# An immediate for the quarter turn of 768 sines, in place of a [128,1] operand

## The chip, the cores and the metric

The kernel runs on one core of one Trainium2 chip. The metric is device microseconds of one execution of the program, as the median of several runs. The time before was 840.31 us (three runs, 839.6 to 840.46). The sets of rounds ran on different chips, so each time is set against the kernel before in its own rounds.

In the profile the engines are called PE (TensorE, matmuls), PEld (TensorE's weight loads), DVE (VectorE), ACT (ScalarE), POOL (GpSimd) and SP (SyncE, whose queue issues most DMAs). L359 is line 359 of the kernel's file. "idle before, releaser" is the time an engine stood before an instruction, and what ended most of it.

## The reference

```python
def _attn_ref(x, filt_r, filt_i):                  # x: 8 x 3008 x 256
    X = np.fft.rfft(x, axis=1)
    Y = X * (filt_r + 1j * filt_i)[None, :, :]
    return np.fft.irfft(Y, n=x.shape[1], axis=1).astype(np.float32)

def _moe_ref(x, w_in, w_out, alpha):               # x: 24064 x 256, 2048 hidden
    h = x @ w_in
    s = np.sin(alpha * h)
    g = h + s * s / (alpha + 1e-09)
    return (g @ w_out).astype(np.float32)
```

A spectral filter along the sequence is followed by a two-layer network whose activation is the "snake" function. As sin² is (1 − cos)/2, the kernel needs the cosine of the scaled hidden value, and takes it as the sine of that value plus a quarter turn.

## The kernel before

The spectral filter of a batch is three stages of matmuls with table matrices. Stage 1 makes `pa` from x. Stage 2 makes `pb`, a product with the filter, and `pc`. Stage 3 makes `pd`. Each of these results stands in PSUM until ACT or DVE evicts it: `pa` to `t`, `pb` to `xf`, `pc` to `g`, `pd` to `y`. For batches 1 to 7 they all share a pool of two PSUM buffers (`fps`). Of the evictions to `t`, `g` and `y`, every third goes to the DVE and two thirds to ACT.

The network works on chunks of up to 512 tokens. A chunk has eight steps. A step holds four hidden matmuls (`ph`, two tiles of 128x512), a piece of the next batch's spectral work, and eight output matmuls (`po`) of the chunk before.

```python
    fps = pool("fps", 2, PSUM)
    hps = pool("hps", 4, PSUM)
    ops = pool("ops", 2, PSUM)
    # ... cut ...
    def evac(dst, src, on_act=None):
        flip[0] = (flip[0] + 1) % 3
        if flip[0] if on_act is None else on_act:
            marks["act"] = nc.scalar.copy(out=dst, in_=src)
        else:
            marks["dve"] = nc.vector.tensor_copy(out=dst, in_=src)
    # ... cut ...
    quarter = cpool.tile([128, 1], FP32)
    nc.vector.memset(quarter, float(np.pi / 2))
    # ... cut: in hidden(k, jb), after the two matmuls into ps ...
        cs = cospool.tile([128, 512], FP32, name=f"cos_{k}_{jb}", tag="c")
        nc.scalar.activation(out=cs[:, 0:n], in_=ps[:, 0:n], func=AFT.Sin, bias=quarter)
        marks["snake"] = nc.vector.scalar_tensor_tensor(
            out=v[k][:, jb, 0:n], in0=cs[:, 0:n], scalar=-1.0, in1=ps[:, 0:n],
            op0=ALU.add, op1=ALU.subtract)
    # ... cut: the main loop ...
        for j in range(8):
            if k < len(chunks):
                hidden(k, 2 * j)
                hidden(k, 2 * j + 1)
            if k == 0:
                weights_out(j)
            while pending and pending[0][0] <= step:
                pending.pop(0)[2]()                       # the spectral pieces
            if k > 0:
                n_half = 2 * (chunks[k - 1][2] // 128)
                for u in range(n_half * j // 8, n_half * (j + 1) // 8):
                    project(k - 1, u)                     # eight output matmuls
            step += 1
```

The program is traced in this order, and a scheduler then decides the order of each engine's instructions, by its own estimate of how long each takes.

Of the kernel before, what the change touches and what calls it, by code (L numbers as in the profile page):

```python
# [10 lines left out]
FP32 = mybir.dt.float32  # L11
AFT = mybir.ActivationFunctionType
# [42 lines left out]
def kernel(  # L55
# [10 lines left out]
    nc = tc.nc  # L66
# [17 lines left out]
    def pool(name, bufs, space=None):  # L84
        kw = {} if space is None else {"space": space}
        return ctx.enter_context(tc.tile_pool(name=name, bufs=bufs, **kw))

    cpool = pool("consts", 1)
# [149 lines left out]
    warm = cpool.tile([128, 1], FP32)  # L238
    nc.vector.memset(warm, 0.0)
    nc.scalar.activation(out=warm, in_=warm, func=AFT.Sin)  # L240
    quarter = cpool.tile([128, 1], FP32)
    nc.vector.memset(quarter, float(np.pi / 2))

    first = spectral(0)
    for _, piece in first[:8]:
# [12 lines left out]
    for i in range(2):  # L258
        al_row.append(opool.tile([128, 2, C], FP32, name=f"al_row_{i}", tag="o"))
        for h in range(2):  # L260
            nc.scalar.dma_start(
                out=al_row[i][64 * h:64 * h + 1].rearrange("p a b -> p (a b)"),
                in_=moe_alpha.rearrange("(k a j) -> k a j", k=4, a=1)[2 * i + h])
# [9 lines left out]
    for g in range(4):  # L273
        for k, filt in enumerate((filt_r, filt_i)):
            for q in range(2):
                off, step = ((6 * g) * C, C) if q == 0 else ((N1 - 6 * g) * C, -C)
                ins = nc.gpsimd.dma_start(
                    out=f_t[k][32 * q:32 * q + 32, 6 * g:6 * g + 6, :],
                    in_=bass.AP(tensor=filt.tensor, offset=filt.offset + off,
                                ap=[[N1 * C, 32], [step, 6], [1, C]]))  # L280
# [18 lines left out]
    ps = fps.tile([128, 512], FP32, name="ps_rec", tag="f")  # L299
# [24 lines left out]
    for i in range(4):  # L324
        for cb in range(2):
            behind(nc.vector.tensor_tensor(
                out=w1[:, cb, 512 * i:512 * i + 512], in0=w_in32[:, cb, 512 * i:512 * i + 512],
# [21 lines left out]
    def hidden(k, jb):  # L349

        _, c0, n = chunks[k]
        if jb == 0:
            v[k] = vpool.tile([128, 16, 512], FP16, name=f"v_{k}", tag="v")
        ps = hps.tile([128, 512], FP32, name=f"ph_{k}_{jb}", tag="h")
        for cb in range(2):
            nc.tensor.matmul(out=ps[:, 0:n], lhsT=w1[:, cb, jb * 128:jb * 128 + 128],  # L356
                             rhs=y_cols[:, cb, c0:c0 + n], start=(cb == 0), stop=(cb == 1))
        cs = cospool.tile([128, 512], FP32, name=f"cos_{k}_{jb}", tag="c")
        nc.scalar.activation(out=cs[:, 0:n], in_=ps[:, 0:n], func=AFT.Sin, bias=quarter)  # L359
        marks["snake"] = nc.vector.scalar_tensor_tensor(  # L360
            out=v[k][:, jb, 0:n], in0=cs[:, 0:n], scalar=-1.0, in1=ps[:, 0:n],
            op0=ALU.add, op1=ALU.subtract)
# [49 lines left out]
    for k in range(len(chunks) + 1):  # L412
# [7 lines that stand above are left out]
                pending.pop(0)[2]()  # L420
# [3 lines that stand above are left out]
                    project(k - 1, u)  # L424
            step += 1
# [31 lines left out]
```

## Time and profile before

| | before |
|---|---|
| time | 840.31 us |
| PE busy | 799.2 us, 95% of the span |
| ACT busy | 674.7 us, 80% |
| DVE busy | 628.4 us, 75% |
| cosine of 128x512, mean | 690 ns |

The page of the kernel before: busy time of the engines, the chain of work that ended last, and three of the costliest groups (count, busy us, mean ns of one, then the idle time before them).

```profile
PE 799.2 (95%) x5793; PEld 544.1 (65%) x5793; DVE 628.4 (75%) x1120; ACT 674.7 (80%) x1200; POOL 28.3 (3%) x55
PE 82%; DMA 7%; DVE 4%; ACT 4%; issue 2%; SPq 0%; POOL 0%; ACTq 0%; DVEq 0%; POOLq 0%
...
L360 DVE SCALAR_TENSOR_TENSOR v<-cos,ph 128x512 f16<-128x512 f32 (+1 forms) x768 | 483.8, 671 | 148.1 <-ACT cos L359 147.1
L359 ACT ACTIVATE cos<-ph,quarter 128x512 f32<-128x512 f32 (+1 forms) x768 | 480.6, 680 | 103.9 <-PE ph L356 101.6
L371 PE MATMUL po<-w,v 128*128 128x256 f16 x3008 | 401.3, 273 | 4.2 <-DVE w L339 4.2
```

TensorE sets the time: it is 82% of the chain. ACT waits 101.6 us for `ph`, so it has time left. The groups split by form show the cost of the operand. All three have 128x512 results from PSUM on ACT; only the first reads a [128,1] operand.

```profile
L359 ACT ACTIVATE cos<-ph,quarter 128x512 f32<-128x512 f32 x704 | 446.9, 690 | 94.4 <-PE ph L356 92.1 <-DVE v L360 1.1
L183 ACT CAST xf<-pb 128x512 f16<-128x512 f32 x96 | 56.6, 591 | 8.8 <-DMA t<-d 5.7 <-DVE p L187 2.0 <-PE pb L180 1.0
L377 ACT COPY o<-po 128x512 f32<-128x512 f32 x92 | 54.9, 597 | 8.5 <-PE po L371 7.4
```

Busy time does not tell how near TensorE is to its own limit, for its matmuls overlap: the `po` above has a mean of 273 ns, yet the next one starts 109 ns after it. The Trainium skill says so too ("Perfetto Trace Analysis", section "Identifying the Most-Contended Engine": matmul busy share is not a good measure). This document therefore uses a sum that is not a view of the profile. For every matmul, take the time to the start of the next one on TensorE, less the median of that time for matmuls of the same result (109 ns for `po`, 216 ns for `ph`). Where this is over 25 ns it is called a *delay*. Summed from 80 us after the start, when the start-up is over, the delays before are 13.7 us. Of these, 4.8 us stand before `pc`, in 23 places, and 5.7 us before `pa`. That sum is the most that a faster ACT or DVE could gain after the start-up; 1.7 us of it is one wait for a load. The view of TensorE's waits, over the same stretch, lists only 2.6 us, because a modelled matmul end hides most of a short delay.

Here is one delay before `pc`, in the timeline of the kernel before (start us, length us, engine, line, operation, tiles, count; in brackets the idle time).

```profile
200.84 2.65 DVE L360 SCALAR_TENSOR_TENSOR v<-cos,ph 128x512 f16<-128x512 f32 x4 [0.31 <-ACT cos L359]
...
203.24 1.03 PE L356 MATMUL ph<-y,w 128*128 128x512 f16 x4
203.41 0.75 DVE L187 TENSOR_TENSOR p<-xf,filt 128x512 f16<-128x512 f16 x2
203.88 1.26 ACT L359 ACTIVATE cos<-ph,quarter 128x512 f32<-128x512 f32 x2 [0.65 <-PE ph L356]
204.07 0.68 DVE L137 CAST g<-pc 128x512 f16<-128x512 f32 x1
204.11 0.38 PE L180 MATMUL pb<-t,d_t 128*128 128x256 f16 x2
204.32 0.49 PE L371 MATMUL po<-w,v 128*128 128x256 f16 x3
204.68 1.27 DVE L360 SCALAR_TENSOR_TENSOR v<-cos,ph 128x512 f16<-128x512 f32 x2
204.81 0.60 PE L199 MATMUL pc<-p,e_t 128*128 128x256 f16 x4
```

Three `po` start at 204.32; at 109 ns each TensorE could start `pc` at 204.65. It starts at 204.81, right after the DVE's eviction of `g` (204.07 + 0.68) frees the buffer. That eviction had queued behind the products (`p`), the products behind the snakes (`v`) of two pairs, which end at 203.49, and these snakes had waited 0.31 us for a cosine. So a shorter cosine should pull this chain forward.

### The profile page before, as it was taken

What the parts mean: (1) busy time and instruction counts of PE and PEld (TensorE: products, weight loads), DVE (VectorE), ACT (ScalarE), POOL (GpSimd) and SP (SyncE); (2) the same over time, 40 slices, a digit from 0 to 9 for tenths busy, and PEclk for the clock granted to TensorE, in tenths of its full rate; (3) what the DMA queues carried; (4) which work ended last, traced back from release to release, by engine and by line L of the source; (5) the groups of instructions that cost most, each with busy time, mean ns of one, the idle gap of its engine ahead of it and who ended that gap; (6) DMA issues with size and microseconds to landing.
All of it is one profiled execution on the core that took longest, in us unless ns stands there. A gap on an engine that the chain in (4) does not pass through costs nothing.

```text
span 839.2 us, 16120 instructions
## 1 busy us (share of the span) xinstructions
PE 799.2 (95%) x5793; PEld 544.1 (65%) x5793; DVE 628.4 (75%) x1120; ACT 674.7 (80%) x1200; POOL 28.3 (3%) x55
## 2 busy tenths in 40 slices
PE   6748999999999999999999999999999999999996
PEld 2324676667776676666776677666767677666674
DVE  3658786777877787777877788777877778777772
ACT  4546897888878898888888888888988988788873
POOL 3210000000000000000000000000000000000000
PEclk9978999999999999999999999999999999999999
DMA  9985845184344734367242763447343343421111
GB/s 216 219 252 116 190 98 130 48 182 106 88 133 82 181 86 98 88 128 167 66 126 61 168 136 81 117 87 171 91 97 94 98 113 82 115 57 38 38 39 45
DMA packets 93495, 94.98 MB, mean 113 GB/s; under 512 B 8084, under 2 KB 82852, under 8 KB 93416
## 3 DMA queue, kind: packets, MB, share of 16 engines
q1 hardware_dynamic: 84784, 75.02, 34.4%
q0 software_dynamic: 6704, 18.09, 12.4%
q10 hardware_dynamic: 1928, 0.86, 0.5%
q8 instruction: 45, 0.74, 0.4%
q14 instruction: 34, 0.28, 0.1%
HBM read 58.02 MB, written 49.81 MB: 128 GB/s over the span
## 4 chain that ended last, share of the span: by engine, by line
PE 82%; DMA 7%; DVE 4%; ACT 4%; issue 2%; SPq 0%; POOL 0%; ACTq 0%; DVEq 0%; POOLq 0%
PE ph L356 35%; PE po L371 35%; PE pc L199 5%; PE pa L157 4%; PE pd L219 2%; DMA t<-d 2%; PE pb L180 2%; ACT cos L359 2%; DMA d<-t 1%; DMA w_out<-in_moe_w_out_dram 1%; DVE v L360 1%; DVE p L187 1%; DMA d<-g 1%; ACT t L135 1%; DMA filt<-in_filt_r_dram 1%
## 5 line engine op out<-in xcount | busy, mean ns | idle before, releaser
L360 DVE SCALAR_TENSOR_TENSOR v<-cos,ph 128x512 f16<-128x512 f32 (+1 forms) x768 | 483.8, 671 | 148.1 <-ACT cos L359 147.1
L359 ACT ACTIVATE cos<-ph,quarter 128x512 f32<-128x512 f32 (+1 forms) x768 | 480.6, 680 | 103.9 <-PE ph L356 101.6
L371 PE MATMUL po<-w,v 128*128 128x256 f16 x3008 | 401.3, 273 | 4.2 <-DVE w L339 4.2
L356 PE MATMUL ph<-y,w 128*128 128x512 f16 (+1 forms) x1536 | 391.3, 376 | 0.3 <-ACT y L135 0.2
L371 PEld LDWEIGHTS <-v 128*128 128x128 f16 x3008 | 289.0, 98 | 80.7 <-issue 8.9
L356 PEld LDWEIGHTS <-w 128*128 128x128 f16 x1536 | 150.6, 98 | 102.8 <-issue 5.5
L187 DVE TENSOR_TENSOR p<-xf,filt 128x512 f16<-128x512 f16 x192 | 72.1, 418 | 6.2 <-ACT xf L183 5.4
L377 ACT COPY o<-po 128x512 f32<-128x512 f32 x96 | 56.5, 589 | 9.8 <-PE po L371 7.4
L183 ACT CAST xf<-pb 128x512 f16<-128x512 f32 x96 | 56.6, 591 | 8.8 <-DMA t<-d 5.7
L135 ACT CAST t<-pa 96x512 f16<-96x512 f32 x89 | 50.0, 588 | 16.4 <-PE pa L157 16.4
L199 PE MATMUL pc<-p,e_t 128*128 128x256 f16 x384 | 59.9, 276 | 2.9 <-DVE p L187 1.5
L219 PEld LDWEIGHTS <-t 96*128 96x128 f16 x512 | 35.5, 98 | 39.0 <-DMA t<-d 11.8
L157 PE MATMUL pa<-x,wf_t 94*96 94x512 f16 x128 | 47.6, 410 | 9.7 <-DMA x<-in_x_dram 5.8
L219 PE MATMUL pd<-wi_t,t 96*128 96x94 f16 x512 | 42.3, 207 | 11.1 <-DMA t<-d 10.6
L135 ACT CAST y<-pd 128x376 f16<-128x376 f32 x82 | 38.7, 474 | 12.2 <-PE pd L219 12.2
L199 PEld LDWEIGHTS <-e_t 128*128 128x128 f16 x384 | 37.7, 99 | 15.7 <-issue 7.5
L180 PE MATMUL pb<-t,d_t 128*128 128x256 f16 x192 | 38.2, 283 | 3.5 <-DMA t<-d 2.4
L135 ACT CAST g<-pc 128x512 f16<-128x512 f32 x64 | 38.7, 605 | 2.2 <-PE pc L199 1.9
L137 DVE CAST y<-pd 128x376 f16<-128x376 f32 x46 | 25.2, 548 | 19.3 <-PE pd L219 19.1
L137 DVE CAST t<-pa 96x512 f16<-96x512 f32 x39 | 26.7, 684 | 16.8 <-PE pa L157 16.1
L180 PEld LDWEIGHTS <-d_t 128*128 128x128 f16 x192 | 18.7, 101 | 25.4 <-DMA t<-d 4.5
L118 POOL DMA_DIRECT2D x<-in_x_dram x32 | 16.6, 522 | 504.6 <-PE pa L157 494.0
(29 smaller groups left out, 86.1 us busy)
## 6 DMA issues: line engine op xcount, KB each, us to landing
d<-t SPq DMA_DIRECT2D x32, 384.0 KB
d<-g SPq DMA_DIRECT2D x64, 192.0 KB
t<-d SPq DMA_DIRECT2D x32, 384.0 KB
x<-in_x_dram POOLq DMA_DIRECT2D x32, 376.0 KB, 7.2
t<-d SPq DMA_DIRECT2D x60, 192.0 KB
out_dram<-o SPq DMA_DIRECT2D x72, 94.0 KB
w_in<-in_moe_w_in_dram POOLq DMA_DIRECT2D x2, 1024.0 KB, 9.0
w_out<-in_moe_w_out_dram POOLq DMA_DIRECT2D x1, 2048.0 KB, 12.4
```

The lines of the kernel that those rows point to most:

```text
L135: marks["act"] = nc.scalar.copy(out=dst, in_=src)
L157: marks["pe"] = nc.tensor.matmul(out=ps[0:NK, :], lhsT=wf_t, rhs=st["x"][ch][:, n0:n0 + 2, :], start=True, stop=True)
L180: nc.tensor.matmul(out=ps[:, i, :], lhsT=d_t[:, s, :], rhs=st["t2"][s // 6][:, s % 6, :], start=True, stop=True)
L183: nc.scalar.copy(out=xf, in_=ps)
L187: marks["prod", u] = nc.vector.tensor_tensor(out=pt, in0=xf, in1=f_t[k][:, 2 * u:2 * u + 2, :], op=ALU.mult)
L199: nc.tensor.matmul(out=ps[:, i, :], lhsT=e_t[:, k, 2 * w + i, :], rhs=pr[k][:, i, :], start=(k == 0), stop=(k == 1))
L219: nc.tensor.matmul(out=psv[:, i, :], lhsT=st["t4"][:, 4 * half + i, cb * 128:cb * 128 + 128], rhs=wi_t, start=True, stop=True)
L356: nc.tensor.matmul(out=ps[:, 0:n], lhsT=w1[:, cb, jb * 128:jb * 128 + 128], rhs=y_cols[:, cb, c0:c0 + n], start=(cb == 0), stop=(cb == 1))
L359: nc.scalar.activation(out=cs[:, 0:n], in_=ps[:, 0:n], func=AFT.Sin, bias=quarter)
L360: marks["snake"] = nc.vector.scalar_tensor_tensor(out=v[k][:, jb, 0:n], in0=cs[:, 0:n], scalar=-1.0, in1=ps[:, 0:n], op0=ALU.add, op1=ALU. ...
L371: nc.tensor.matmul(out=pso[k][:, t % 2, :], lhsT=v[k][:, jb, 128 * t:128 * t + 128], rhs=w2[:, jb, :], start=(jb == 0), stop=(jb == 15))
L377: nc.scalar.copy(out=o[:, 0:nb, :], in_=pso[k][:, 0:nb, :])
```

## The change

The operand becomes an immediate, a number within the instruction, so that the instruction no longer reads a [128,1] tile, and the memset goes.

```diff
-    quarter = cpool.tile([128, 1], FP32)
-    nc.vector.memset(quarter, float(np.pi / 2))
...
-        nc.scalar.activation(out=cs[:, 0:n], in_=ps[:, 0:n], func=AFT.Sin, bias=quarter)
+        nc.scalar.activation(out=cs[:, 0:n], in_=ps[:, 0:n], func=AFT.Sin, bias=float(np.pi / 2))
```

The two built programs also differ in their order, although the source order is the same.

## The prediction

> **What bounds the kernel.** The page gives PE 799 of 839 us (95%), ACT 675 (80%), DVE 628 (75%). I summed matmul columns by stretch (groups by form): from 200 to 700 us they fill 96 to 97% of the time at 2400 columns per us. Matmuls there follow each other every 216 ns (512 columns) or 109 ns (256), both also the medians of the run, so TensorE runs at its own rate. The chain of waits says the same: PE is 82% of it, the cosine (ACT, L359) 1.7%.
>
> **What the change does.** It removes the [128,1] operand from 768 ACTIVATEs and one memset. The cosine lasts 687 ns (median); evictions of the same 128x512 from PSUM by the same engine without such an operand last 588 ns. Starts of two cosines in a row are some 575 ns apart, of two evictions 465. The Trainium skill ("ScalarE: Activation LUTs", section "What ACT_TABLE_LOAD costs") says a [128,1] pointer operand adds about 93 ns to an ACTIVATE; the 100 ns between cosine and eviction agrees, though these are different instructions. I expect 585 to 595 ns for the cosine, and some 75 us less ACT busy time, to about 600.
>
> **How much is on the critical path.** Little. I took every matmul start that came over 25 ns later than the usual distance. Before 80 us such delays are the start-up: loads, the half clock granted there, and the wait for the output weights (the DVE stood 4.5 us for that load). The cosine sets none of it but some tenths. After 80 us they come to only 13 us in all: 4.8 us before stage 2's second matmuls (pc), which wait for the DVE's eviction of g; about 5.3 us before stage 1 (pa), waiting for ACT's evictions of y and t queued behind a pair of cosines; 1.7 us for one DMA. They are 0.16 to 0.39 us each. A cosine 0.1 us shorter moves the DVE's chain (snake, products, g) up by 0.1 us and an ACT eviction behind two cosines by 0.2 us. Estimate: 2.5 us less before pc, 2.5 to 3 before pa: 5 to 6 us gained at most.
>
> **What it moves.** The built orders differ: the scheduler thinks the cosine shorter. On the DVE some 25 evictions, mostly of y, now stand behind a pair of snake instructions (1.28 us) where they stood before it. Most harm nothing, as the next use of their buffer is two steps off. Where stage 1 of the next batch overlaps (the y of pd_8 or pd_9 in three batches, and two t), two buffers are shared and the next pa may stand 0.5 to 1 us: an estimate of 2 to 4 us given back. On ACT and PE a few evictions and single matmuls swap near 58 to 95 us and at the overlaps; six stores go behind loads. I expect little of these.
>
> **Predicted:** 838 us, range 834 to 841. Faster by over 2%: 1%; within 2%: 98%; slower by over 2%: 1%.
>
> **What would show it.** Cosine median near 590 ns; ACT busy near 600 us; PE busy share unchanged at 95 to 96%; ACT's wait for ph (101.6 us before) longer by most of the 75 us; PE's delays before pc smaller; delays of 0.5 us or more before some pa, waiting for y on the DVE; start-up to 66 us unchanged.
>
> **What would make it wrong.** The immediate costs as much as the operand (no change at all); the moved evictions cost more than a few us (842 to 846); the granted clock, 0.5 in parts of the start-up, shifts; or delays after 80 us vanish entirely (828), which would still be within 2%.

## The result, and the profile after

The changed kernel took 840.04 us (four runs, 839.21 to 841.37), against 840.38 us of the kernel before (four runs). The ratio is 0.9994, with a 95% interval of 0.9972 to 1.0016. All ratios in this document are made from runs of both kernels in the same rounds; they are not quite the ratio of the medians quoted (e1 below: 0.9919, 0.9908 by the medians).

The page of the changed kernel, the lines that answer to those above:

```profile
PE 799.8 (96%) x5793; PEld 544.2 (65%) x5793; DVE 628.1 (75%) x1119; ACT 613.0 (73%) x1200; POOL 28.3 (3%) x55
PE 83%; DMA 7%; ACT 4%; issue 3%; DVE 2%; POOL 0%; SPq 0%; ACTq 0%; DVEq 0%; POOLq 0%
...
L358 DVE SCALAR_TENSOR_TENSOR v<-cos,ph 128x512 f16<-128x512 f32 (+1 forms) x768 | 484.0, 672 | 164.0 <-ACT cos L357 163.5
L357 ACT ACTIVATE cos<-ph 128x512 f32<-128x512 f32 (+1 forms) x768 | 411.6, 589 | 153.9 <-PE ph L354 152.5
L369 PE MATMUL po<-w,v 128*128 128x256 f16 x3008 | 400.9, 273 | 2.6 <-DVE w L337 2.6
```

And its cosine of 128x512 alone, from the groups by form:

```profile
L357 ACT ACTIVATE cos<-ph 128x512 f32<-128x512 f32 x704 | 383.6, 598 | 140.0 <-PE ph L354 138.6
```

The cosine fell from 690 to 598 ns, to the level of a plain eviction, and ACT's busy time by 61.7 us. Most of that became waiting: ACT's wait for `ph` grew from 101.6 to 152.5 us. TensorE's delays after 80 us went only from 13.7 to 13.1 us. The same delay before `pc` in the changed kernel's timeline:

```profile
201.82 1.03 PE L354 MATMUL ph<-y,w 128*128 128x512 f16 x4
201.89 0.75 DVE L187 TENSOR_TENSOR p<-xf,filt 128x512 f16<-128x512 f16 x2
202.45 1.08 ACT L357 ACTIVATE cos<-ph 128x512 f32<-128x512 f32 x2 [0.83 <-PE ph L354]
202.56 0.68 DVE L137 CAST g<-pc 128x512 f16<-128x512 f32 x1
202.68 0.38 PE L180 MATMUL pb<-t,d_t 128*128 128x256 f16 x2
202.90 0.38 PE L369 MATMUL po<-w,v 128*128 128x256 f16 x2
203.16 1.27 DVE L358 SCALAR_TENSOR_TENSOR v<-cos,ph 128x512 f16<-128x512 f32 x2
203.30 0.60 PE L199 MATMUL pc<-p,e_t 128*128 128x256 f16 x4
```

Measured from the start of `ph`, the DVE's `g` starts 0.74 us later here (202.56 − 201.82) and 0.83 us later before (204.07 − 203.24). So the chain did come 0.09 us earlier, by as much as the cosine is shorter. But only two `po` stand between `pb` and `pc`, not three. TensorE has 0.109 us less work to fill the wait with, and the delay stays: 0.18 us in place of 0.16. The gain may thus be there and have been given back by the new order. The experiments ask whether that is so, how large both sides are, and which engine's order gives it back.

### The profile page after: what moved, and what is told of

It reads as the page before. It is cut to its first block, busy times and chain, and to the rows that moved or that the text cites. A ratio compares the mean times of both kernels' runs of the same rounds, so it can differ in the third digit from the quotient of the medians.

```text
span 837.2 us, 16122 instructions
## 1 busy us (share of the span) xinstructions
PE 799.8 (96%) x5793; PEld 544.2 (65%) x5793; DVE 628.1 (75%) x1119; ACT 613.0 (73%) x1200; POOL 28.3 (3%) x55
## 4 chain that ended last, share of the span: by engine, by line
PE 83%; DMA 7%; ACT 4%; issue 3%; DVE 2%; POOL 0%; SPq 0%; ACTq 0%; DVEq 0%; POOLq 0%
PE po L369 36%; PE ph L354 35%; PE pc L199 4%; PE pa L157 3%; ACT cos L357 2%; PE pd L219 2%; PE pb L180 2%; DMA t<-d 1%; DMA w_out<-in_moe_w_out_dram 1%; DMA d<-g 1%; DMA d_t<-d_tbl 1%; DVE p L187 1%; DMA x<-in_x_dram 1%; DMA filt<-in_filt_i_dram 1%; ACT t L135 1%
## 5 line engine op out<-in xcount | busy, mean ns | idle before, releaser
L357 ACT ACTIVATE cos<-ph 128x512 f32<-128x512 f32 (+1 forms) x768 | 411.6, 589 | 153.9 <-PE ph L354 152.5
L219 PE MATMUL pd<-wi_t,t 96*128 96x94 f16 x512 | 43.4, 208 | 11.1 <-DMA t<-d 10.9
L157 PEld LDWEIGHTS <-wf_t 94*96 94x96 f16 x128 | 16.6, 129 | 19.6 <-issue 9.9
```

The costliest lines, as they stand in the source:

```text
L157: marks["pe"] = nc.tensor.matmul(out=ps[0:NK, :], lhsT=wf_t, rhs=st["x"][ch][:, n0:n0 + 2, :], start=True, stop=True)
L219: nc.tensor.matmul(out=psv[:, i, :], lhsT=st["t4"][:, 4 * half + i, cb * 128:cb * 128 + 128], rhs=wi_t, start=True, stop=True)
```

## The experiments

Theory A: the shorter cosine is worth several us, and the scheduler's new order gives them back. Rival B: these delays hang on a ring of DVE and TensorE work, and the cosine's length hardly matters.

| run | order | cosine | time, us | before in the same rounds | ratio, 95% interval | delays after 80 us: all | before pc | before pa |
|---|---|---|---|---|---|---|---|---|
| before | old | operand | 840.38 | | | 13.7 | 4.8 | 5.7 |
| changed | new | immediate | 840.04 | 840.38 | 0.9994, 0.9972–1.0016 | 13.1 | 4.6 | 6.0 |
| e1 | old | immediate | 833.29 | 841.03 | 0.9919, 0.9904–0.9934 | 6.1 | 1.9 | 2.2 |
| e2 | new | operand | 848.62 | 841.03 | 1.0095, 1.0079–1.0111 | 21.8 | 7.5 | 10.5 |
| e3 | old | two operands | 853.63 | 841.03 | 1.0152, 1.0138–1.0165 | 25.9 | 11.1 | 10.3 |
| e4 | new, g on ACT | immediate | 836.07 | 841.03 | 0.9949, 0.9937–0.9962 | 10.9 | 0.1 | 5.9 |
| e5 | PE old, rest new | immediate | 839.67 | 841.77 | 0.9969, 0.9947–0.9992 | 12.1 | 2.0 | 6.8 |
| e6 | PE new, rest old | immediate | 840.28 | 841.77 | 0.9979, 0.9957–1.0001 | 12.7 | 4.4 | 5.5 |
| e7 | pieces in the middle | immediate | 835.11 | 841.77 | 0.9917, 0.9896–0.9938 | 7.5 | 0.6 | 5.0 |
| e8 | pieces last | immediate | 834.67 | 841.77 | 0.9909, 0.9886–0.9932 | 7.4 | none | 4.3 |
| e9 | as e8 | operand | 837.1 | 840.89 | 0.9955, 0.994–0.997 | 10.5 | none | 7.2 |
| e10 | old, g on ACT | immediate | 831.14 | 840.89 | 0.9889, 0.9869–0.9909 | 5.5 | none | 2.1 |
| e11 | DVE new, rest old | immediate | 837.73 | 841.57 | 0.9957, 0.9939–0.9975 | 11.2 | 2.1 | 6.1 |
| e12 | ACT and DMA new, rest old | immediate | 834.89 | 841.57 | 0.9924, 0.9908–0.994 | 7.4 | 2.0 | 3.3 |

All of them gave correct results. The delays come from one profiled execution each. They account for the times: in these fourteen profiles the span goes from 829.8 to 852.0 us, but the span less the delays only from 823.1 to 826.0 us.

### e1 and e2: the two parts of the change, one at a time

To change the operand without the order, the kernel is scheduled first and the 768 cosines are replaced in the finished program. Every wait and every place in the order stay. For e1 the source is the kernel before:

```diff
+    for f in nc.m.functions:                      # after the scheduler
+        for b in f.blocks:
+            listed = b.instructions
+            for n, i in enumerate(listed):
+                if ...:                           # a Sin of a ph tile: 768 of them
+                    listed[n] = copy.replace(i, ins=(i.ins[0], ImmediateValue(
+                        dtype=FP32, value=float(np.pi / 2)), *i.ins[2:]))
```

For e2 the source is the changed kernel, with the memset of `quarter` and one read of it by an early ACTIVATE kept, and the operand put in. The order of e1 equals that of before on every engine. The order of e2 equals that of the changed kernel, but for the memset and the place of one DMA issue in the start-up.

> The order of before on every engine, with the immediate put into the 768 cosines after the scheduler has run. Theory A (the shorter cosine does shorten TensorE's waits, and the scheduler's new order gives that back: it puts the second matmuls of stage 2 and of stage 1 one or more output matmuls of 109 ns earlier): cosine median 590 ns, TensorE's delays after 80 us down from 13.7 to 7 to 10 us, time 3 to 6 us under before (834.5 to 837.5). Rival B (those waits do not hang on the cosine but on a ring of DVE and TensorE work): delays 12.5 to 13.7 us, time 839 to 841, as the changed kernel.

> The order of the changed kernel, with the [128,1] operand put back into the 768 cosines after the scheduler has run. Theory A: cosine median 687 ns, delays after 80 us of 17 to 20 us, each of stage 2's waits 0.28 in place of 0.18 us, time 842.5 to 846. Rival B: delays near 13 us, time 839 to 841.

Measured: 833.29 us for e1 and 848.62 us for e2. Theory A holds in both, and both sizes were larger than expected. In the old order the immediate is worth 7.7 us (841.03 − 833.29). With the operand the new order costs 7.6 us (848.62 − 841.03). From the ratios and their intervals one gets 6.8 us (5.6 to 8.1) and 8.0 us (6.6 to 9.3), so each size is known to little better than 1 us. The timeline of e1 at the delay shown above:

```profile
199.41 1.03 PE L356 MATMUL ph<-y,w 128*128 128x512 f16 x4
...
200.04 1.09 ACT L359 ACTIVATE cos<-ph 128x512 f32<-128x512 f32 x2 [0.83 <-PE ph L356]
200.15 0.68 DVE L137 CAST g<-pc 128x512 f16<-128x512 f32 x1
...
200.49 0.49 PE L371 MATMUL po<-w,v 128*128 128x256 f16 x3
200.75 1.27 DVE L360 SCALAR_TENSOR_TENSOR v<-cos,ph 128x512 f16<-128x512 f32 x2
200.89 0.60 PE L199 MATMUL pc<-p,e_t 128*128 128x256 f16 x4
```

`g` again starts 0.74 us after `ph`, as in the changed kernel. But three `po` stand before `pc`, as before, so `pc` comes 0.40 us after their first start and the delay is 0.07 us. The 23 delays before `pc` sum to 1.9 us.

### e3: a longer cosine

The old order once more, with the scale of 1 given as a second [128,1] operand, put in after the scheduler in the same way.

```diff
-   ins=(ph, quarter, ImmediateValue(1.0), ...)
+   ins=(ph, quarter, one, ...)                    # one: a [128,1] tile of 1.0
```

> The order of before, and the cosine's scale of 1 as a second [128,1] operand. Theory A: cosine median some 780 ns, each of stage 2's 0.16 us waits becomes about 0.25 us and stage 1's 0.29 about 0.5, delays after 80 us of 19 to 24 us, time 845 to 852. Rival B: time 839 to 841 and delays near 13 us, while ScalarE is busy some 745 us.

Measured: 853.63 us, a little over the expected range, with delays of 25.9 us (19 to 24 expected). The group by form:

```profile
L361 ACT ACTIVATE cos<-ph,quarter,one 128x512 f32<-128x512 f32 x704 | 510.9, 785 | 52.0 <-PE ph L358 48.6 <-DVE w L341 0.5
```

With no, one and two operands the cosine takes 598, 690 and 785 ns, so each operand costs 92 and 95 ns. In the same order of work the time goes 833.29, 841.03, 853.63: the second operand costs 12.6 us and the first 7.7. Two things in the traces go with the larger second step: 34 delays stand before `pc` in place of 23, and two cosines in a row now start 676 ns apart (585 before), so that the second snake of a pair waits for its cosine and the pair lasts 1.36 us in place of 1.27 or 1.28. How much each makes is not shown. Rival B falls.

### e4: the eviction of g moved to ACT

```diff
-                evac(st["g"][:, i0:i0 + 2, :], ps, i0 != 2 if b == 0 else None)
+                evac(st["g"][:, i0:i0 + 2, :], ps, i0 != 2 if b == 0 else True)
```

> The changed kernel with all of stage 2's evictions of g on ScalarE for batches 1 to 7 (before: every third on the DVE). ScalarE has time left after the change. Theory A says the wait of 0.18 us before stage 2's second matmuls, 4.4 us in all, ends with the DVE's eviction of g and so goes; if nothing else comes in its place, time 835 to 837. If ScalarE's queue takes over (cosine pair, xf, g, and o every fourth step), the wait comes back behind an eviction of ScalarE and the time is 839 to 842.

Measured: 836.07 us, inside the lower of the two ranges. The delays before `pc` are gone but for 0.1 us, so they did hang on the DVE's eviction of `g`. The scheduler also moved the `po` here: none is left between `pb` and `pc` in the 23 places, so nothing fills a wait there, and still there is none. Those before `pa` are what they were in the changed kernel (5.9 us).

### e5 and e6: TensorE's order alone

Here the changed kernel is scheduled with a recorded order of some engines. Each instruction is put behind its neighbour by a dependency without a semaphore, which orders the issue only. It adds seven lines ahead of the kernel body, so line numbers shift by seven.

```diff
+    for engine, order in PINNED.items():
+        made = [...]                               # that engine's instructions as traced
+        for n in range(1, len(order)):
+            tc.add_manual_dep(made[order[n]], made[order[n - 1]].name, ...)   # NoSync
```

> The changed kernel with TensorE's order pinned to that of before; DVE, ACT and the DMA queue keep the changed kernel's order. Theory P (what gives the gain back is TensorE's order: pc after two output matmuls in place of three, pa after six in place of seven): 833 to 836, delays after 80 us of 6 to 8 us. Rival D (as predicted before: it is the DVE's evictions of y standing behind a pair of snakes): 838 to 841, delays of 11 us or more with waits for y on the DVE.

> The changed kernel with TensorE's own (changed) order, and DVE, ACT and the DMA queue pinned to the order of before. Theory P: 838.5 to 841, delays after 80 us of 12 to 13.5 us. Rival D: 833 to 836.

Measured: 839.67 us for e5 and 840.28 us for e6. Theory P was right for e6 and wrong for e5; rival D was right for e5 and wrong for e6. So neither alone is the cause: each half of the new order is enough to lose most of the gain, and the two losses do not add. The columns by result show what belongs to which. Of the orders, the delays before `pc` follow TensorE's alone: 4.4 us with the new one (e6), 2.0 with the old (e5). Those before `pa` rise from 2.2 us (e1) with either half: to 5.5 us in e6 and 6.8 us in e5.

### e11 and e12: the other engines, apart

> The changed kernel with only the DVE in its changed order; TensorE, ACT and the DMA queue pinned to the order of before. Theory V (the cost of the non-TensorE part, some 6 us of delays in the run that left only TensorE in the old order, is the DVE's evictions of y and t behind a pair of snakes): delays after 80 us of 10 to 12 us with waits before pa of some 0.44 us, time 837.5 to 840.5. Rival S (it is ACT's order, o and t swapped, or the stores put behind loads): 6 to 7.5 us, 832.5 to 835.

> The changed kernel with ACT and the DMA queue in their changed order; TensorE and DVE pinned to the order of before. Theory V: delays after 80 us of 6 to 7.5 us, time 832.5 to 835. Rival S: delays of 10 to 12 us, time 837.5 to 840.5.

The edit is that of e5, with other engines named. Measured: 837.73 us and delays of 11.2 us with the DVE's new order alone, 834.89 us and 7.4 us with the new order of ACT and of the DMA queue. Theory V was right for both. So the larger part of what e5 lost is the DVE's doing, some 5.1 us of delays (11.2 − 6.1), and the orders of ACT and the DMA queue cost at most 1.3 us of delays. The times agree in direction: by the ratios e11 lies 0.38% over e1 and e12 only 0.05%. The timeline of e11 where the evictions of stage 3 meet stage 1:

```profile
172.41 0.33 PE L226 MATMUL pd<-wi_t,t 96*128 96x94 f16 x4
172.58 0.38 PE L164 MATMUL pa<-x,wf_t 94*96 94x512 f16 x1
172.80 0.71 PE L376 MATMUL po<-w,v 128*128 128x256 f16 x5
172.81 1.28 DVE L365 SCALAR_TENSOR_TENSOR v<-cos,ph 128x512 f16<-128x512 f32 x2 [0.89 <-ACT cos L364]
173.15 0.58 ACT L142 CAST t<-pa 96x512 f16<-96x512 f32 x1
173.78 0.38 PE L164 MATMUL pa<-x,wf_t 94*96 94x512 f16 x1 [0.27 <-ACT t L142]
...
174.01 0.54 DVE L144 CAST y<-pd 128x376 f16<-128x376 f32 x1
```

The same place in e12, where the DVE has its old order:

```profile
172.41 0.33 PE L226 MATMUL pd<-wi_t,t 96*128 96x94 f16 x4
172.58 0.38 PE L164 MATMUL pa<-x,wf_t 94*96 94x512 f16 x1
172.78 0.55 DVE L144 CAST y<-pd 128x376 f16<-128x376 f32 x1 [0.86 <-PE pd L226]
172.80 0.71 PE L376 MATMUL po<-w,v 128*128 128x256 f16 x5
...
173.25 1.28 DVE L365 SCALAR_TENSOR_TENSOR v<-cos,ph 128x512 f16<-128x512 f32 x2
173.38 0.38 PE L164 MATMUL pa<-x,wf_t 94*96 94x512 f16 x1
```

In e12 the DVE evicts `y` at once, and the second `pa` starts 0.58 us after the five `po` began, a delay of 0.04 us. In e11 `y` stands behind the pair of snakes and ends at 174.55. The second `pa` gets the other buffer, whose eviction by ACT ends at 173.73, and it starts 0.98 us after the `po` began, a delay of 0.44 us. The DVE was free before both: in e12 `y` starts at 172.78, in e11 the snakes start at 172.81, so all that differs is which of the two stands first in its order. In e11 nine delays before `pa` are 0.42 or 0.44 us, one is 0.62 us, and one before `ph` is 0.94 us; in e1 there is no delay of any of these sizes.

The changed kernel has the same order on the DVE there, but seven `po` in place of five, which fill 0.22 us of it and leave a delay of 0.22 us. That is one reason why the two losses before `pa` do not add. That it is the only one is not shown.

### e7, e8 and e9: an order that the source sets

Can the source ask for a better order? The spectral piece of each step can be traced later in the step. e7 traces it after four of the eight output matmuls (the output function gets a half as a further argument), e8 after all eight:

```diff
-            while pending and pending[0][0] <= step:
-                pending.pop(0)[2]()
             if k > 0:
                 n_half = 2 * (chunks[k - 1][2] // 128)
                 for u in range(n_half * j // 8, n_half * (j + 1) // 8):
                     project(k - 1, u)
+            while pending and pending[0][0] <= step:
+                pending.pop(0)[2]()
```

> The changed kernel with each step's spectral piece traced after four of the eight output matmuls of the step, so that pc and pa come later for TensorE by the source and not by the scheduler's clock. Theory P: the waits before pc go, those before pa shrink, delays after 80 us of 3 to 6 us, time 830 to 834, under both kernels and no slower than the order of before with the immediate (833.3). If the rest of the delays doesn't hang on this order: 837 to 841.

> The changed kernel with each step's spectral piece traced after all eight output matmuls of the step, just ahead of the next hidden matmuls. Theory P: as with four, 830 to 835, unless the cosine's own input (ph) then comes later behind pb, pc or pa and ScalarE's queue makes new waits: then 836 to 842, with waits before ph or po.

> The order of the run with the pieces traced last, with the [128,1] operand put back into the cosines after the scheduler has run. Tells whether the operand is worth a fixed amount or only what stands in an order's waits. If it is worth what it was in the other two orders (7.7 to 8.6 us): 842 to 844. If this order has taken the waits before pc out of the cosine's reach, only those before pa are left (some 20 of 0.2 us each): 836.5 to 840, delays after 80 us of 9 to 12 us.

Measured: 835.11 us for e7, a little over its range and with delays of 7.5 us over the 3 to 6 expected, and 834.67 us for e8, inside the range of theory P. By the intervals of their ratios both are faster than both original kernels. They have few or no delays before `pc`. e9, with the operand put back into the order of e8, took 837.1 us. By the two ratios the operand costs 0.46% there (0.9955 − 0.9909), an estimate of 3.9 us; by the delays 3.1 us (10.5 − 7.4). In the old order the same operand cost 7.7 us. That is inside the range expected if only the delays before `pa` are left to the operand (836.5 to 840 us). So a shorter cosine has no fixed worth: it is worth what stands in the waits of the order in use.

### e10: two of the edits together

The kernel before with all of `g` on ACT, scheduled with the operand; the immediate is put in afterwards, as in e1. This joins e1 and e4. The scheduler moves some `po` here too, so TensorE's order is not quite that of e1.

> Scheduled with the operand, immediate put in after, and all of g's evictions of batches 1 to 7 on ScalarE. The order of before with the immediate still had 1.9 us of waits for the DVE's g before pc. Those go: 830.5 to 833.5, delays after 80 us of 3.5 to 5 us. If ScalarE's queue then holds up y or t by an eviction more: 833 to 837.

Measured: 831.14 us, 1.1% under before, with delays of 5.5 us where 3.5 to 5 were expected. No delay before `pc` is left. Of the remaining 5.5 us, 3.1 us stand before `pd`, nearly all of it one wait of 2.9 us for a load. It has the lowest time, though its interval overlaps those of e1 and e8, so that it is faster than these is not shown. Swapping operands in a finished program is a tool rather than a way to write kernels. e8 reaches 834.67 us by moving two lines.

## Why the prediction was right or wrong

- **The time** was right: 838 us was predicted with a range of 834 to 841, and 840.04 was measured, within 2%.
- **The bound** was right. TensorE's share and its busy time stayed (799.2 and 799.8 us), and of 61.7 us less ACT time no more than 7.7 us came through to the time, even with the order held still (e1).
- **The cost of the operand** was right in kind: 100 ns were expected from the evictions, 92 ns measured. The median of the cosine came out at 597 ns, against 585 to 595. ACT's busy time fell to 613 us and not to 600, partly because each cosine lost 92 ns and not 100, and partly because busy time counts overlapping instructions once: the lengths of ACT's instructions, summed, fell by 70.2 us.
- **Where the gain could lie** was right: in the 13.7 us of short delays ("13 us in all", the prediction said). Its size was too small. "5 to 6 us gained at most" measured 7.7 us in time and 7.6 us in delays (13.7 − 6.1) once the order was held still (e1). The term for `pc` was 2.5 and measured 2.9 us (4.8 − 1.9). The term for `pa` was 2.5 to 3 and measured 3.5 us (5.7 − 2.2). The rest, delays before `pd`, `ph` and `pb`, was not in the sum.
- **What the order gives back** was right in kind and too small: "2 to 4 us" measured 7.0 us of delays (13.1 − 6.1). The DVE's part, evictions of `y` behind a pair of snakes, is real (e11). Alone it makes 5.1 us of delays, mostly in nine pieces of about 0.4 us, where 0.5 to 1 us in some five places had been expected.
- **The step that failed** is "On ACT and PE a few evictions and single matmuls swap near 58 to 95 us and at the overlaps; ... I expect little of these." TensorE's swaps were not few: 23 `pc` and 23 `pa` come one `po` earlier. They keep the delays before `pc` at 4.6 us (e5 against the changed kernel: 2.0 and 4.6), and with the others' order held old they lose nearly everything by themselves (e6, delays of 12.7 us). For ACT and the DMA queue the guess was about right (e12).
- **The sign that was named** for the give-back, delays of 0.5 us or more before some `pa`, did not appear in the changed kernel: the longest delay before `pa` is 0.28 us. Where the timelines above were taken, TensorE's new order filled half of the delay; that it did so everywhere is not shown. "PE's delays before pc smaller" did not appear either (4.8 to 4.6 us), as TensorE's new order took it back (2.0 us with the old one, e5). That the total came near is partly luck: the gain was too small by some 2 us and what was given back by some 3 to 5 us, and the two have opposite signs.

## What to carry to other kernels

A change to an instruction's operand can also change the order that a scheduler makes, and the new order may take back what the instruction gains: compare the two orders before costing the change, and count how many instructions move, not only where. To separate the two, hold the order and change the instruction, then hold the instruction and change the order; here two effects of 7 to 8 us each lay behind a difference of 0.3 us. On an engine that is the bound, a 0.1 us matmul placed before or after a wait is worth as much as 0.1 us taken off the work that ends the wait: with the same cosine, three `po` before `pc` left 0.07 us of delay and two left 0.18.

## What the Trainium skill lacked or had wrong

- "ScalarE: Activation LUTs", section "What ACT_TABLE_LOAD costs": its formulas give 613 ns with immediates and 707 ns with a pointer bias for 512 elements (186 and 280 ns plus 0.833 ns for each). This kernel, reading PSUM and writing SBUF, shows means of 598 and 690 ns, some 16 ns less. The 93 ns that it gives for each [128,1] pointer operand agree with the runs: 92 ns for the first and 95 ns for the second (598, 690, 785 ns).
- "Perfetto Trace Analysis", section "Identifying the Most-Contended Engine", is right that matmul busy share tells little. But the share of weight loads, one of the two measures that it names in its place, told little here either: 65% before, 65% after and 66% in e1, with 7.7 us between the first and the last. The loads' busy time stayed (544.1, 544.2 and 543.8 us), so the share moved only because the span did. The other measure, MFU, was not worked out. The distance from one matmul's start to the next, against its usual value, did show it, and the section does not name that measure.
- The same page, section "Optimization Strategy", says that a gap that repeats on the engine that should be saturated can mean too few buffers. The repeated delay of 0.16 us before `pc` is such a gap, as `pc` waits for one of two shared PSUM buffers. The page does not say that the order on the bounding engine can shrink or close the gap with the same buffers and the same cosine (delays before `pc` of 4.6 us in the changed kernel, 2.0 us with TensorE's old order in e5, none in e8, where the orders of all engines differ).
- No page tells that an operand's form can change a scheduled program's order, or how much that may cost: 7.6 us here (e2).
